# An attention and expert kernel: the work between the two expert stages moved, and the gate's iterations cut in parts

## The chip, the cores and the metric

The kernel runs on one core of one Trainium2 chip. The metric is the device time of one execution in microseconds (us); the median of three runs counts. One more execution was profiled, and all rows below are from it. The engines are called as the profile calls them: PE is TensorE (matrix products), DVE is VectorE, ACT is ScalarE, POOL is GpSimd, and SP only starts transfers. PEld is the loading of weights into TensorE, which runs beside its matmuls.

## What is computed

The reference has three parts in a row, on 1152 tokens of 512 values. Attention with a learned bias gives x; a dense layer with softplus follows; then comes a mixture of eight experts, whose gate is a matrix of probabilities that is normalized by rows and by columns eight times.

```python
# dense layer: w_in 512 x 2048, w_out 2048 x 512
h = x @ w_in
x = softplus(h) @ w_out
# experts: w1[e] 512 x 1024, w2[e] 1024 x 512
P = np.exp(x @ w_gate - (x @ w_gate).max())      # 1152 x 8
for _ in range(8):
    P /= P.sum(1, keepdims=True) + 1e-09
    P /= P.sum(0, keepdims=True) + 1e-09
    P *= N / E
out = 0
for e in range(8):
    out += P[:, e:e + 1] * (np.maximum(x @ w1[e], 0.0) @ w2[e])
```

## The kernel before

Everything is in fp32. A product is made of three matmuls on a high and a low part of each operand (`TRIPS`), so each operand must first be split: ACT copies it to the high part, and DVE or POOL subtracts that to get the low part.

The dense layer and the experts are cut into 40 **units** of 256 hidden columns. Units 0 to 7 are the dense layer (`U1` is 8); units 8 to 39 are the experts, four units (`UE`) for each, so that units 8 to 11 are expert 0. All emission is by hand: `unit(u)` writes the instructions of one unit in the order in which each engine will run them, and each engine runs its own list in order. Tiles and semaphores only add the waits.

The tokens are two chunks of 512 (c = 0 and 1) and a rest of 128. A unit of the experts has these steps on PE. First come seven block products of x with w1 in the order 1, 2, 6, 7, 5, 3, 4 (a Strassen scheme over 2 x 2 blocks; product 6 needs the block sum S2, product 7 needs S3, 5 needs S1, 3 needs S4, and 4 needs the plain block A22). Then `up_last` does the 128 rest tokens, `down(u, 0)` and `down(u, 1)` multiply the hidden values with w2, four matmul groups (i = 0 to 3) each, and `down_last` does the rest. After each group DVE adds the result to the output tile `acc` (`evac`). PSUM has eight banks: two called `t`, one `tail`, one `pv`, and two double ones called `s`, which hold the sums of `down`.

The block sums are needed in the experts alone, and they are sums of the dense layer's output, so they can only be made when unit 7 ends. `x_next` and `finish_x` do this: `x_mix` adds two blocks of 128 x 512, on DVE or POOL, and `x_split` makes the high part on ACT and the low part on DVE or POOL. `x_part` splits a plain block (A11, A12, A22). `rows_to_x` transposes the rest tokens on PE and splits them.

The gate is a list of closures: logits, transposes to tokens, the maximum, the exponential, and eight iterations `columns(it)`. Each iteration is a matmul with a matrix of ones on PE, into bank `pv`, and nine small DVE instructions on tiles `prob` (128 x 72), `r8` and `r9`. `ask()` takes the next closure off the list. It is called six times in each unit from unit 8 on, so that the 17 closures are used up in units 8 to 10. From expert 1 on (unit 12), `acc` is first scaled by expert 0's probability (`weigh`, nine DVE instructions).

POOL mainly prepares the weights: `mix` makes sums of weight blocks and `parts` splits weights (ACT copies, L613; POOL subtracts, L614). `JOBS` says after which step of a unit the weights of the next unit are made.

Of the kernel before, what the change touches and what calls it, by code (L numbers as in the profile page):

```python
# [24 lines left out]
E = 8  # L25
# [62 lines left out]
def attention_moe_moe_kernel(ctx: ExitStack, tc, qT, kT, vN, wpos, w_in, w_out, w_gate, e_w1, e_w2,  # L88
# [421 lines left out]
    def experts(m0, accp, xr):  # L510
# [247 lines left out]
        def down(u, c):  # L758
            w = wd(u).rearrange("p o (t f) -> p o t f", t=2)
            order = (0, 2, 1, 3) if u == U1 - 1 else (0, 1, 2, 3)  # L760
            t = [ps2("sum") for _ in range(2)]
            for i, k in enumerate(order):
# [11 lines left out]
                if i == 1 and u >= U1:  # L774
                    ask()
# [3 lines left out]
        def down_last(u):  # L779
            w = wd(u).rearrange("p o (t f) -> p o t f", t=2)  # L780
            r, n, t = bank("pv"), 0, h["last"]
# [4 lines left out]
            evac(u, 2, 0, r)  # L786
            if u == U1 - 1:
                finish_x()
# [19 lines left out]
        def x_next(c, k):  # L808

            if c == 0:  # L810
                xsrc[0] = acc[0]
                x_part("A11" if k < 2 else "A12", k % 2)
                return
            xsrc[1] = acc[1]
            if k == 2:
                x_mix("S1", 0, nc.gpsimd)
            elif k == 3:
                for n in range(2):
                    x_mix("S3", n, nc.gpsimd)
                x_mix("S2", 0)  # L820
                x_mix("S1", 1)
                x_mix("S2", 1)

        def finish_x():
            for k in range(2):
                x_split("S2", k, nc.vector)
            for name in ("S3", "S1"):
# [60 lines left out]
        def exps():  # L888
            mb = bank("pv")
# [3 lines left out]
            rows()  # L893

        def rows():
            nc.vector.tensor_reduce(pool["r9"], pool["prob"], axis=AX.X, op=ALU.add)
            nc.vector.tensor_scalar(pool["r9"], pool["r9"], 1e-9, None, ALU.add)
            nc.vector.reciprocal(pool["r9"], pool["r9"])
            nc.vector.tensor_tensor(out=pool["prob"], in0=pool["prob"], in1=pool["r9"].rearrange("p (t o) -> p t o", o=1).to_broadcast(
                [128, NTOK // 128, E]), op=ALU.mult)  # L900

        def columns(it):
            cs = bank("pv")
            nc.tensor.matmul(cs[:, 0:NTOK // 128 * E], ones, pool["prob"].rearrange("p t e -> p (t e)"), start=True, stop=True)
            nc.vector.tensor_reduce(pool["r8"], cs[:, 0:NTOK // 128 * E].rearrange("p (t e) -> p e t", e=E), axis=AX.X, op=ALU.add)
            nc.vector.tensor_scalar(pool["r8"], pool["r8"], 1e-9, None, ALU.add)
            nc.vector.reciprocal(pool["r8"], pool["r8"])
            nc.vector.tensor_scalar(pool["r8"], pool["r8"], float(NTOK / E), None, ALU.mult)
            nc.vector.tensor_tensor(out=pool["prob"], in0=pool["prob"], in1=pool["r8"].rearrange("p (o e) -> p o e", o=1).to_broadcast(
                [128, NTOK // 128, E]), op=ALU.mult)  # L910
            if it < 7:
                rows()

        def weigh():

            for t in range(NTOK // 128):
                d = acc[t // 4][:, t % 4]
                nc.vector.tensor_scalar(d, d, pool["prob"][:, t, 0:1], None, ALU.mult)

        gate = []  # L920
        for c in range(3):
# [258 lines left out]
```

## Time and profile before

| | us |
|---|---|
| median of 3 runs (1289.26 to 1289.4) | 1289.33 |
| the profiled execution's own time | 1289.71 |
| its span on the core | 1287.8 |
| PE busy in the span | 1203.0 (93%) |
| DVE busy | 841.1 (65%) |
| POOL busy | 581.6 (45%) |
| ACT busy | 488.3 (38%) |

The span is the time from the first to the last instruction of the profiled execution, and 1.9 us lie around it. Times in the rows count from the start of the span. A row's last part in square brackets is how long the engine sat idle before the instruction, and on what it had waited. [...]

### The profile page before, as it was taken

The numbers are of one execution on the slowest core, as the hardware profiler recorded it, in microseconds if no ns is written. First come the engines' busy times: TensorE is split into PE (matmuls) and PEld (weight loads), VectorE is DVE, ScalarE is ACT, GpSimd is POOL, SyncE is SP. The second block draws the span as 40 slices with busy tenths as digits, with TensorE's granted clock in tenths as the row PEclk, the third lists the DMA queues.
The fourth block names the chain that finished last, engine by engine and source line by source line (L and its number), as shares of the span: only waits on it lengthen the run. The fifth ranks groups of instructions, "written<-read, shape, count | busy, mean of one in ns | idle before, by whom it ended". The sixth has DMA issues, their size and how long they took to land.

```text
span 1287.8 us, 19090 instructions
## 1 busy us (share of the span) xinstructions
PE 1203.0 (93%) x7460; PEld 1011.3 (79%) x7460; DVE 841.1 (65%) x1502; ACT 488.3 (38%) x855; POOL 581.6 (45%) x452
## 2 busy tenths in 40 slices
PE   5775989999999998988999999999999999999998
PEld 4675868887887885766888888888888888888887
DVE  8883678764777766377756556656566566565665
ACT  7773766784332333322323223223232232232321
POOL 1122677655444549333534534544445345444440
PEclk9887999999999998999999999999999999999999
DMA  4998636603222311110111111111111111111101
GB/s 92 147 195 170 182 84 205 184 2 98 81 83 77 108 46 33 33 41 26 48 49 50 50 33 50 50 33 49 50 50 49 33 50 50 33 49 50 33 1 74
DMA packets 75148, 90.85 MB, mean 71 GB/s; under 512 B 17332, under 2 KB 51764, under 8 KB 75060
## 3 DMA queue, kind: packets, MB, share of 16 engines
q1 hardware_dynamic: 74772, 89.36, 25.6%
q8 instruction: 58, 0.95, 0.3%
q14 instruction: 30, 0.25, 0.1%
q10 hardware_dynamic: 288, 0.30, 0.1%
HBM read 74.45 MB, written 15.19 MB: 70 GB/s over the span
## 4 chain that ended last, share of the span: by engine, by line
PE 77%; DVE 11%; DMA 4%; POOL 3%; issue 2%; ACT 2%; SPq 1%; POOLq 0%; DVEq 0%; ACTq 0%
PE sum L770 31%; PE t L676 16%; PE pv L784 4%; PE tail L744 3%; PE pv L676 3%; PE tail L676 3%; PE t L691 3%; PE op L449 2%; PE pac L198 2%; PE pv L691 1%; PE tail L691 1%; PE sps L361 1%; PE tp L412 1%; DVE m L188 1%; DVE acc L800 1%
## 5 line engine op out<-in xcount | busy, mean ns | idle before, releaser
L614 POOL TENSOR_TENSOR wu<-f,wu 128x1024 fp32r<-128x1024 f32 x72 | 172.8, 2400 | 445.0 <-ACT wu L613 444.5
L770 PE MATMUL sum<-wd,h 128*128 128x512 f32 x1536 | 367.1, 395 | 1.5 <-DVE acc L800 1.5
L770 PEld LDWEIGHTS sum<-wd,h 128*128 128x128 f32 x1536 | 285.9, 190 | 59.1 <-DVE acc L800 2.0
L802 DVE SCALAR_TENSOR_TENSOR acc<-sum,prob,acc 128x512 f32<-128x512 f32 x224 | 168.2, 751 | 137.4 <-PE sum L770 137.4
L676 PE MATMUL t<-room,wu 128*128 128x512 f32 x512 | 142.4, 390 | 2.7 <-ACT v L726 2.7
L676 PE MATMUL t<-x,wu 128*128 128x512 f32 x448 | 122.6, 390 | 0.0
L676 PEld LDWEIGHTS t<-room,wu 128*128 128x128 f32 x512 | 95.9, 188 | 22.9 <-ACT v L726 3.1
L614 POOL TENSOR_TENSOR wd<-f,wd 128x1024 fp32r<-128x1024 f32 x40 | 96.0, 2399 | 36.5 <-ACT wd L613 36.5
L726 ACT ACTIVATE v<-t 128x512 f32<-128x512 f32 x32 | 19.1, 597 | 242.9 <-PE t L676 242.9
L198 PE MATMUL pac<-bw,m 128*128 128x64 bf16 (+1 forms) x1920 | 72.5, 204 | 32.6 <-DVE bw L171 12.3
L676 PEld LDWEIGHTS t<-x,wu 128*128 128x128 f32 x448 | 84.2, 188 | 17.5
L198 PEld LDWEIGHTS <-m 128*128 128x128 bf16 (+1 forms) x1920 | 69.1, 109 | 35.8 <-issue 26.6
L770 PE MATMUL sum<-h,wd 128*128 128x512 f32 x384 | 94.1, 397 | 2.7 <-DVE acc L800 2.0
L770 PEld LDWEIGHTS sum<-h,wd 128*128 128x128 f32 x384 | 69.9, 188 | 21.6 <-DVE acc L800 7.1
L613 ACT ACTIVATE wu<-f 128x1024 fp32r<-128x1024 f32 x72 | 75.8, 1053 | 15.6 <-DVE f L595 15.6
L579 POOL TENSOR_SCALAR f<-f 128x512 f32<-128x512 f32 x32 | 61.8, 1939 | 28.3 <-DVE f L578 28.0
L800 DVE TENSOR_TENSOR acc<-sum,acc 128x512 f32<-128x512 f32 x80 | 54.6, 687 | 27.7 <-PE sum L770 27.2
L378 ACT ACTIVATE p<-p,sm 128x576 f32<-128x576 f32 x72 | 55.7, 773 | 31.8 <-DVE sm L374 20.7
L711 ACT ACTIVATE hl<-tail 128x256 fp32r<-128x256 f32 x40 | 15.3, 384 | 130.6 <-PE tail L753 130.6
L374 DVE CUSTOM_DVE_ANT_0 p<-sps,bias 128x576 f32<-128x576 f32 x72 | 54.0, 750 | 15.9 <-DMA bias<-wt 10.8
L711 ACT ACTIVATE h<-pv 128x512 fp32r<-128x512 f32 x40 | 23.9, 598 | 103.1 <-DVE pv L695 102.8
L695 DVE TENSOR_TENSOR tail<-tail,v 128x512 f32<-128x512 f32 x32 | 22.4, 699 | 60.9 <-PE tail L676 60.3
(188 smaller groups left out, 2180.4 us busy)
## 6 DMA issues: line engine op xcount, KB each, us to landing
f<-in_e_w_dram SPq DMA_DIRECT2D x128, 256.0 KB, 2.9
raw<-in_w_in_dram SPq DMA_DIRECT2D x16, 512.0 KB, 3.7
raw<-in_w_out_dram SPq DMA_DIRECT2D x16, 512.0 KB, 3.6
wt<-extra SPq DMA_DIRECT2D x10, 512.0 KB, 7.7
raw<-in_qT_dram SPq DMA_DIRECT2D x16, 288.0 KB, 4.9
raw<-in_kT_dram SPq DMA_DIRECT2D x16, 288.0 KB, 4.5
bias<-wt SPq DMA_DIRECT2D x16, 288.0 KB, 4.6
bias<-wt SPq DMA_DIRECT2D x16, 256.0 KB, 4.4
```

What stands on the lines that cost most here:

```text
L198: nc.tensor.matmul(pt[0:n, g], lhs, win(w, (k * (ng + 1) + gw) * NC, [[(ng - gw) * NC, 2], [1, NC]]), start=(k == 0), stop=(k == 2))
L374: nc.vector.tensor_tensor_reduce(out=p.rearrange("p (a j) -> p a j", a=2), in0=sps[:, :, 0:288], in1=bias.rearrange("p (a j) -> p a j", a= ...
L378: nc.scalar.activation(p, p, AF.Exp, bias=sm[:, o:o + 1], scale=-1.0, accum_out=sm[:, 2 + o:3 + o])
L579: nc.gpsimd.tensor_scalar(t, t, F64_MIN, F64_MAX, ALU.max, ALU.min)
L613: nc.scalar.activation(w[:, 0], src, AF.Copy)
L614: nc.gpsimd.tensor_tensor(out=w[:, 1], in0=src, in1=w[:, 0].bitcast(F32), op=ALU.subtract)
L676: nc.tensor.matmul(z[n], wu(u)[:, a, o:o + 128], xs[xn][b][j], start=(k == 0), stop=(k == 5))
L691: nc.tensor.matmul(zz, wu(u)[:, a, o:o + 128], xs[f"A{c + 1}{k // 2 + 1}"][b][k % 2], start=(k == 0 and n == 0), stop=(k == 3 and n == 2))
L770: nc.tensor.matmul(s, lhs, rhs, start=(n == 0), stop=(n == 5))
L784: nc.tensor.matmul(r, t[:, b, 128 * f:128 * f + 128], w[:, a, f], start=(n == 0), stop=(n == 5))
L800: nc.vector.tensor_tensor(out=d, in0=o, in1=d, op=ALU.add)
L802: nc.vector.scalar_tensor_tensor(out=d, in0=o, scalar=pool["prob"][:, t, e:e + 1], in1=d, op0=ALU.mult, op1=ALU.add)
```

## The change

There are three edits, and some small ones that go with them.

**The block sums.** All of `x_mix` is now on DVE, and its pieces stand between the last evictions of unit 7 and the first of unit 8, in the order in which the products need them: S2, S3, S1, S4. All low parts of the sums are made on DVE too; A22 stays on POOL. The rest tokens' sum of unit 7 goes into a bank of `s` (`sumr`) instead of `pv`, and it is evicted later. `rows_to_x` comes after product 3 instead of product 5, as one instruction on each engine instead of four. The weights of unit 8 are made earlier in unit 7 (`FIRST`).

**The gate.** Each iteration is three closures instead of one, each with a named place in a unit: r0 to r2 around `up_last`, a0 to a3 after the four evictions of `down(u, 0)`, and b0 to b3 after those of `down(u, 1)`. The intermediate values stand in the bank `pv` instead of SBUF. The multiplication by N / E is folded into the one that follows it. The last iteration now comes in unit 12.

**The weighting** of `acc` in unit 12 is nine ACT instructions instead of nine on DVE, each group just ahead of the sums that need it.

```diff
         def down(u, c):
+            weigh(u, c)
...
                 evac(u, c, k, s)
                 convert(1)
-                if i == 1 and u >= U1:
-                    ask()
+                ask(u, "ab"[c] + str(i))
...
         def down_last(u):
-            r, n, t = bank("pv"), 0, h["last"]
+            weigh(u, 2)
+            r, n, t = bank("pv") if u != U1 - 1 else ps2("sumr")[:, 0], 0, h["last"]
...
-            evac(u, 2, 0, r)
             if u == U1 - 1:
-                finish_x()
+                pool["sumr"] = r
+            else:
+                evac(u, 2, 0, r)
...
             if k == 2:
-                x_mix("S1", 0, nc.gpsimd)
+                x_mix("S1", 0)
+            elif k == 1:
+                x_mix("S2", 0)
             elif k == 3:
-                for n in range(2):
-                    x_mix("S3", n, nc.gpsimd)
-                x_mix("S2", 0)
                 x_mix("S1", 1)
                 x_mix("S2", 1)
-
-        def finish_x():
...
+                for n in range(2):
+                    x_split("S2", n, nc.vector)
+                for n in range(2):
+                    x_mix("S3", n)
+
+        def finish_x(n):
+            if n == 1:
                 for k in range(2):
-                    x_split(name, k)
-            for k in range(2):
-                x_mix("S4", k)
-                x_split("S4", k, nc.vector)
-            for k in range(2):
-                x_part("A22", k)
+                    x_split("S3", k, nc.vector)
+                evac(U1 - 1, 2, 0, pool.pop("sumr"))
+            elif n == 2:
+                for k in range(2):
+                    x_split("S1", k, nc.vector)
+            elif n == 6:
+                for k in range(2):
+                    x_mix("S4", k)
+                for k in range(2):
+                    x_split("S4", k, nc.vector)
+            elif n == 7:
+                for k in range(2):
+                    x_part("A22", k)
+            elif n == 3:
+                rows_to_x()
...
         def columns(it):
...
+            def first():
+                cs["t"] = t = bank("pv")
...
+                nc.tensor.matmul(t[:, 0:NT * E], ones, pool["prob"].rearrange("p t e -> p (t e)"), start=True, stop=True)
+                r8 = t[:, 256:256 + E]
+                nc.vector.tensor_reduce(r8, t[:, 0:NT * E].rearrange("p (t e) -> p e t", e=E), axis=AX.X, op=ALU.add)
+                nc.vector.tensor_scalar(r8, r8, 1e-9, None, ALU.add)
+                nc.vector.reciprocal(r8, r8)
...
+            def second():
...
+                if it < 7:
+                    rows(cs["p"], cs["t"][:, 300:300 + NT])
+
+            def third():
+                if it < 7:
+                    rows_done(cs["p"], cs["t"][:, 300:300 + NT], pool["r9"])
...
+        for it, (n, at) in enumerate(((1, "b"), (2, "r"), (2, "a"), (2, "b"), (3, "r"), (3, "a"), (3, "b"), (4, "r"))):
+            for k, fn in enumerate(columns(it)):
+                gate[n, f"{at}{k}"] = fn
...
+        FIRST = {0: (("mix", 0),), 1: (("high", 0),), 2: (("high", 1),), 3: (("highd", 0),)}
```

How the lists of the engines move is shown at three places. A row has the line, the operation, the tile that is written and those that are read, and the shape.

The first place is DVE from the last evictions of unit 7 into the first products of unit 8. `raw_2551` is S1, `raw_2552` S2, `raw_4620` S3 and `raw_4621` S4; `x_4625`, `room`, `x_4623` and `x_4627` are the low parts of S2, S3, S1 and S4. Before:

```order
L713 TENSOR_TENSOR hl<-tail,hl 128x256
L800 TENSOR_TENSOR acc<-sum,acc 128x512 x4
L651 TENSOR_TENSOR raw_2552<-raw_2551,acc 128x512
L651 TENSOR_TENSOR raw_2551<-acc 128x512
L651 TENSOR_TENSOR raw_2552<-raw_2551,acc 128x512
L800 TENSOR_TENSOR acc<-pv,acc 128x512
L656 TENSOR_TENSOR x_4625<-raw_2552,x_4624 128x512 x2
L651 TENSOR_TENSOR raw_4621<-acc,raw_2552 128x512
L656 TENSOR_TENSOR x_4627<-raw_4621,x_4626 128x512
L651 TENSOR_TENSOR raw_4621<-acc,raw_2552 128x512
L656 TENSOR_TENSOR x_4627<-raw_4621,x_4626 128x512
```

And now:

```order
L651 TENSOR_TENSOR raw_2552<-raw_2551,acc 128x512
L656 TENSOR_TENSOR x_4625<-raw_2552,x_4624 128x512 x2
L651 TENSOR_TENSOR raw_4620<-acc 128x512 x2
L656 TENSOR_TENSOR room<-raw_4620,room 128x512 x2
L802 TENSOR_TENSOR acc<-sumr,acc 128x512
L695 TENSOR_TENSOR tail<-tail,v_6120 128x512
L886 COPY lgt<-pv 8x512
L656 TENSOR_TENSOR x_4623<-raw_2551,x_4622 128x512 x2
L695 TENSOR_TENSOR u_6166<-t,v_6120 128x512
L715 SCALAR_TENSOR_TENSOR h<-tail,h 128x512
L651 TENSOR_TENSOR raw_4621<-acc,raw_2552 128x512 x2
L656 TENSOR_TENSOR x_4627<-raw_4621,x_4626 128x512 x2
```

The sums of S3 (which POOL made) and the low parts of S3 and S1 (also POOL's) have come into this list, and the eviction of the rest tokens has moved behind S3. Above this piece, between the last three evictions of unit 7, stand the first halves of S1 and S2 and the second half of S1.

The second place is POOL over the same stretch, from the high blocks' low parts (`room<-acc`: A11 and A12) to those of A22 (`x_4628`). Before:

```order
L637 TENSOR_TENSOR room<-acc,room 128x512 x4
L614 TENSOR_TENSOR wd_2548<-f_4618,wd_2548 128x1024
L651 TENSOR_TENSOR raw_2551<-acc 128x512
L651 TENSOR_TENSOR raw_4620<-acc 128x512 x2
L656 TENSOR_TENSOR room<-raw_4620,room 128x512 x2
L656 TENSOR_TENSOR x_4623<-raw_2551,x_4622 128x512 x2
L637 TENSOR_TENSOR x_4628<-acc,room 128x512 x2
```

And now:

```order
L637 TENSOR_TENSOR room<-acc,room 128x512 x4
L607 TENSOR_TENSOR f_2550<-f_4617 128x2x2x128
L608 TENSOR_TENSOR f_2550<-f_4617 128x2x128
L609 TENSOR_TENSOR f_2550<-f_4617,f_2550 128x2x128
L610 TENSOR_TENSOR f_2550<-f_2550 128x2x128
L614 TENSOR_TENSOR wu_4615<-f_4617,wu_4615 128x1024
L637 TENSOR_TENSOR x_4628<-acc,room 128x512 x2
```

The seven rows of S1 and S3 are gone. In front of A22 there now stand the weight sums of unit 9 (L607 to L610) and the split of its first weights (L614), which waits for ACT's copy of the same weights; on ACT that copy (L613, `wu_4615<-f_4617`) stands behind the high parts of S4.

The third place is DVE around `up_last` of unit 10, where one gate iteration stands behind product 4 and ahead of the first eviction of `down`. Before:

```order
L695 TENSOR_TENSOR t<-t,u_6641 128x512
L715 SCALAR_TENSOR_TENSOR h<-t,h 128x512
L905 TENSOR_REDUCE r_5177<-pv 128x8
L906 TENSOR_SCALAR r_5177<-r_5177 128x8
L907 RECIPROCAL r_5177<-r_5177 128x8
L908 TENSOR_SCALAR r_5177<-r_5177 128x8
L909 TENSOR_TENSOR prob<-prob,r_5177 128x72
L896 TENSOR_REDUCE r_5176<-prob 128x9
L897 TENSOR_SCALAR r_5176<-r_5176 128x9
L898 RECIPROCAL r_5176<-r_5176 128x9
L899 TENSOR_TENSOR prob<-prob,r_5176 128x72
L715 SCALAR_TENSOR_TENSOR h<-t,h 128x512
L800 TENSOR_TENSOR acc<-sum,acc 128x512 x2
```

And now:

```order
L695 TENSOR_TENSOR t<-t,u_6611 128x512
L715 SCALAR_TENSOR_TENSOR h<-t,h 128x512
L929 TENSOR_REDUCE pv<-pv 128x8
L930 TENSOR_SCALAR pv<-pv 128x8
L931 RECIPROCAL pv<-pv 128x8
L935 SCALAR_TENSOR_TENSOR pv<-prob,pv 128x72
L912 TENSOR_REDUCE pv<-pv 128x9
L913 TENSOR_SCALAR pv<-pv 128x9
L715 SCALAR_TENSOR_TENSOR h<-t,h 128x512
L916 RECIPROCAL r_5176<-pv 128x9
L917 TENSOR_TENSOR prob<-pv,r_5176 128x72
L802 TENSOR_TENSOR acc<-sum,acc 128x512
```

The nine small rows are now eight, with a low part of the hidden values (`h<-t,h`) among them, and all of them read `pv`, the PSUM bank; only the last two write to SBUF. The next iteration's matmul on PE (a0) stands behind the first group of `down(u, 0)` and reads the `prob` that the last small row writes.

## Rows read from the trace of the kernel before

**Rows 1.** Stretch, length, busy PE, PEld, DVE, ACT, POOL, PEclk: units 8 (halved) to 11.

```profile
495.79:521.62 25.83, 18.34 (x75) 12.39 (x74) 19.94 (x27) 11.10 (x21) 18.94 (x14) 0.87 0.13 42
521.62:539.22 17.60, 16.91 (x88) 12.24 (x86) 1.66 (x5) 7.25 (x13) 8.14 (x6) 1.00 0.10 31
539.22:569.62 30.40, 27.30 (x120) 21.55 (x120) 20.47 (x47) 8.22 (x12) 10.50 (x7) 0.94 0.10 35
569.62:602.61 32.99, 27.44 (x123) 21.95 (x122) 27.77 (x70) 6.49 (x10) 10.37 (x7) 0.95 0.10 33
602.61:626.07 23.46, 23.46 (x111) 19.63 (x110) 13.96 (x21) 6.49 (x10) 10.50 (x7) 1.00 0.13 45
```

**Rows 2.** What PE waited for from 478 to 626 us: total, times, longest.

```profile
PE pv L904 <- DVE prob L899: 4.3, 2, 2.5
...
PE pv L877 <- ACT acc L798: 0.7, 1, 0.7
```

**Rows 3.** Timeline of PE: start, duration, instructions, idle time before and its releaser.

```profile
491.57 3.02 PE L770 MATMUL sum<-h,wd 128*128 128x512 f32 x12 [0.76 <-DVE acc L800]
...
501.44 4.39 PE L870 MATMUL pv<-room,gw 128*8 128x512 f32 x12 [2.77 <-DVE acc L800]
...
509.92 1.65 PE L676 MATMUL t<-room,wu 128*128 128x512 f32 x6 [2.71 <-ACT v L726]
...
519.74 0.41 PE L877 MATMUL pv<-ident,lgt 8*128 8x8 f32 x4 [2.02 <-DVE h L715]
...
589.03 0.41 PE L904 MATMUL pv<-prob,ones 128*128 128x72 f32 x2 [2.48 <-DVE prob L899]
```

**Rows 4.** Short stretches behind three waits of PE, columns as in rows 1.

```profile
502.50:504.50 2.00, 2.00 (x6) 0.63 (x5) 1.77 (x2) 1.22 (x3) 2.00 (x2) 0.50 0.04 8
...
520.00:522.00 2.00, 2.00 (x17) 1.94 (x16) 1.67 (x4) 1.62 (x3) 0.00 (x0) 1.00 0.15 50
...
590.50:592.50 2.00, 2.00 (x6) 1.52 (x6) 1.83 (x7) 0.00 (x0) 1.59 (x3) 0.50 0.55 207
```

**Rows 5.** Timeline of DVE and POOL where both work on SBUF.

```profile
495.29 4.22 POOL L651 TENSOR_TENSOR raw<-acc 128x512 f32<-128x512 f32 x3
...
498.30 1.76 DVE L651 TENSOR_TENSOR raw<-acc 128x512 f32<-128x512 f32 x1
...
500.09 0.69 DVE L651 TENSOR_TENSOR raw<-raw,acc 128x512 f32<-128x512 f32 x1
...
586.45 2.34 POOL L614 TENSOR_TENSOR wd<-f,wd 128x1024 fp32r<-128x1024 f32 x1
586.56 0.22 DVE L898 RECIPROCAL r<-r 128x9 f32<-128x9 f32 x1
586.81 2.07 DVE L899 TENSOR_TENSOR prob<-prob,r 128x72 f32<-128x72 f32 x1
```

**Rows 6.** Groups by line and shape, 495.79 to 626.07 us: count, busy us, mean ns.

```profile
L614 POOL TENSOR_TENSOR wu<-f,wu 128x1024 fp32r<-128x1024 f32 x8 | 19.2, 2398 | 56.5 <-ACT wu L613 56.5
...
L613 ACT ACTIVATE wu<-f 128x1024 fp32r<-128x1024 f32 x8 | 8.4, 1052 | 0.0
...
L607 POOL TENSOR_TENSOR f<-f 128x512 f32<-128x512 f32 x5 | 6.4, 1288 | 0.0
...
L637 POOL TENSOR_TENSOR x<-acc,room 128x512 fp32r<-128x512 f32 x2 | 2.8, 1420 | 0.1
...
L896 DVE TENSOR_REDUCE r<-prob 128x9 f32<-128x72 f32 x8 | 1.8, 230 | 0.7 <-ACT prob L892 0.4
...
L905 DVE TENSOR_REDUCE r<-pv 128x8 f32<-128x72 f32 x8 | 1.8, 223 | 0.5 <-PE pv L904 0.5
```

**Rows 7.** Timeline of PE and DVE in unit 11, from the end of product 4.

```profile
612.13 1.59 PE L744 MATMUL tail<-wu,xl 128*128 128x256 f32 x12
...
612.93 1.45 DVE L715 SCALAR_TENSOR_TENSOR h<-t,h 128x512 fp32r<-128x512 f32 x2
...
613.56 2.68 PE L770 MATMUL sum<-wd,h 128*128 128x512 f32 x11
```

More of the change, by code (lines that the diff above doesn't have):

```diff
@@ L892, in exps @@
             nc.scalar.activation(pool["prob"], pool["prob"], AF.Exp, bias=pool["mx"][:, 2:3])
[L893 to L900, printed above, removed]
@@ L902, in columns @@
-        def columns(it):
[L903 to L921, printed above, removed]
-            gate += [lambda c=c: logits(c), lambda c=c: tokens_down(c)]
-        gate += [max_rows, max_all, exps]
-        gate += [lambda it=it: columns(it) for it in range(8)]
+        NT = NTOK // 128
+        def rows(src, r9):
+            nc.vector.tensor_reduce(r9, src, axis=AX.X, op=ALU.add)
+            nc.vector.tensor_scalar(r9, r9, 1e-9, None, ALU.add)
@@ new lines, in weigh, with tokens_max @@
+        def weigh(u, c):
+            if u == U1 + UE:
+                for k in range(4 if c < 2 else 1):
+                    d = acc[c][:, k]
+                    nc.scalar.activation(d, d, AF.Copy, scale=pool["prob"][:, 4 * c + k, 0:1])
+        def tokens_max():
+            tokens_down(2)
+            max_rows()
+        gate = {(0, "p"): lambda: logits(0), (0, "r1"): lambda: tokens_down(0), (0, "a0"): lambda: logits(1),
+                (0, "a2"): lambda: tokens_down(1), (0, "b0"): lambda: logits(2), (0, "b2"): tokens_max,
+                (1, "r1"): max_all, (1, "a0"): exps, (1, "a2"): lambda: rows(pool["prob"], pool["mb"][:, 300:300 + NT]),
+                (1, "a3"): lambda: rows_done(pool["prob"], *[pool["mb"][:, 300:300 + NT]] * 2)}
@@ L997, in jobs @@
                 if U1 <= u + 1 < NU:
-                    for what, k in JOBS.get(n, ()):
+                    for what, k in (JOBS if u >= U1 else FIRST).get(n, ()):
                         weights[what](u + 1, k)
@@ L1033, in unit @@
                 return
-            if u == U1 + UE:
-                while gate:
-                    gate.pop(0)()
-                weigh()
             for n, p in enumerate((1, 2, 6, 7, 5, 3, 4)):
@@ L1040, in unit @@
                 jobs(n)
-                if n == (1 if u == U1 else 3) or n == 6:
-                    ask()
-                if u == U1 and n == 4:
-                    rows_to_x()
+                if n == 1:
+                    ask(u, "p")
+                if u == U1:
+                    finish_x(p)
+            ask(u, "r0")
             up_last(u)
+            ask(u, "r1")
             low()
+            ask(u, "r2")
             load_up()
@@ L1050, in unit @@
             jobs(8)
-            ask()
             turn_last(u)
@@ L1054, in unit @@
             down_last(u)
-            ask()
             load_down()
@@ L1063, in convert, with ask @@
                 weights[what](u, k)
-        def ask():
-            if gate:
-                gate.pop(0)()
+        def ask(u, at):
+            fn = gate.pop((u - U1, at), None)
+            if fn:
+                fn()
         return beside, rest
```

23 lines of the change are left out of this document (16 added, 7 removed).

## The prediction

> **What bounds the kernel now.** I read the stretches first. They show PE without a gap in unit 11: 23.46 us busy of 23.46, at the full clock [rows 1]. From unit 12 to the end the units keep that length, so nothing that lightens another engine there can shorten the run. The place to look is units 8 to 10, which take 25.83 + 17.60 + 30.40 + 32.99 = 106.82 us where three units like unit 11 would take 70.38 [rows 1]. This excess of 36.4 us is all that the change can work on. It has three parts.
>
> - PE stands idle for 7.5 + 0.7 + 3.1 + 5.6 = 16.8 us, the differences of span and busy time [rows 1]. The waits of PE say for whom: before logits it waits 2.77 us for the eviction on DVE that frees bank `pv`; then 2.71 for ACT's copy of product 1, late because ACT stands behind the splits of the block sums; then 2.02 for DVE [rows 3]. In units 9 and 10 it waits for `prob`, 4.3 us in two waits [rows 2].
> - PE has work of its own for the gate: two logits of 12 matmuls, small transposes, ones-matmuls. Eleven matmuls of 512 columns take 2.68 us with the tail [rows 7], so 12 take 2.75 and a product of 6 takes 1.36. With the rest chunk, the transposes of the rest tokens and the ones-matmuls I put all of it at 9.6. This stays.
> - The rest, 36.4 - 16.8 - 9.6 = 10 us, is work at the lower clock. [...] So a long wait is paid again behind it: busy time in a half-clock stretch counts double, and I value one such stretch at 2 us.
>
> **Unit 7's end and the products of unit 8.** I walk through the lists on the old trace's time axis. In the old list, group i = 2 of `down(7, 1)` waits 0.76 us [rows 3] for an eviction that is late because ACT copied weights (1.05 us, [rows 6]) just before the rest tokens' hidden values. That copy now comes earlier in the unit, under products that PE does anyway, and the 0.76 is gained. Product 1 then starts at about 494.9.
>
> The logits no longer wait for the rest tokens' sum, which now has a bank of its own. They run from 497.6 to 500.3, and product 6 wants S2 then. On DVE there stand, ahead of S2's low parts, two evictions, four sums and the splits; one op on 128 x 512 is 0.69 us undisturbed [rows 5].
>
> The price of these ops is open, because POOL works beside them. A sum with both inputs in SBUF took 1.76 us while POOL worked on three sums of its own, and 0.69 alone [rows 5]: up to 1.1 more for each. POOL's list now brings unit 9's weight sums at that time, from 490.8 on: one op of 1.29 us [rows 6] and three on half as much, 3.5 in all. So the disturbance costs nothing at best, and 4 x 1.1 = 4.3 at worst. I take 1.2, two sums that wait for the rest of one POOL op, since POOL's next piece stands still until ACT comes to its copy.
>
> [...]
>
> S2 is then ready at 498.1 and S3 at 500.7, both before PE wants them (500.3, 501.7). From there DVE is behind: eviction of the rest sum, product 2, logits copy, S1's low parts (ready at 504.4, wanted at 503), product 6, a low part, two sums S4, two splits: 19 ops from the second half of S1 on, at 0.65 each with the waits for ACT in between, end at 508.2. Product 3 ends at 508.6 where it would have ended at 505.8.
>
> Next late is A22. ACT copies unit 9's first weights after S4's high parts (to 508.5), POOL splits them (2.4 us, to 510.9), and only then come A22's two low parts (2.8 us with both, [rows 6]; 2.5 undisturbed), to 513.4. Product 4 ends at 514.0 and `up_last` at 515.4. In the old trace `up_last` ends at 521.62 [rows 1]. **This stretch gains 6.2 us**, the 0.76 included. The cover that is gone here is POOL's: before, A22 did not stand behind the weights.
>
> The holes of some 2 us before product 3 and 2.6 before product 4 may lower the clock behind them, as the old waits did. I count one such stretch, **2.0 lost** (bounds: 0, since 2.02 did nothing, and 4).
>
> **The rest of unit 8** loses its wait of 0.7 [rows 2], since the last transposes now come ahead of a matmul group instead of behind everything. One group of transposes (0.34) moves into it. **0.4 gained.**
>
> **Units 9 and 10.** All small ops now read PSUM, or SBUF with one operand only. The old trace shows why that matters: a `prob` update with both operands in SBUF took 2.07 us while POOL split weights, and a reciprocal beside the same POOL op took 0.22 [rows 5]. A small op costs 0.22 to 0.23 us whether its source is PSUM or SBUF [rows 6], so I put no price on PSUM.
>
> [...]
>
> The parts matter where PE waits for `prob`. Between a and b, and between b and the next r, there are 2 us or more of matmuls to spare after the third part. Between r and a there are not. In unit 11 product 4 ended at 612.13; DVE finished the first of two low parts at 613.6 [rows 7]. From there a chain of six small ops (0.26 from one to the next with the wait for itself), one low part (0.6) and two more small ops makes 2.5, to 616.1. The first group of `down` ends 0.4 later than in rows 7 because of the ones-matmul, at 615.3, so PE waits 0.85 there, and about 0.2 for bank `pv` at r0. That is 1.05 in each of units 10 and 11.
>
> Unit 9 gets 23.46 + 0.64 of PE work (maximum, broadcast, one iteration) + 0.2 = 24.3. Unit 10 gets 23.46 + 3 x 0.17 + 1.05 = 25.0. Together 49.3 against 63.4 [rows 1]: **14.1 gained**, waits of 1 us being too short for the lower clock by rows 3 and 4.
>
> **Units 11 and 12** now carry the last iterations. Unit 11 takes 25.0 instead of 23.46, **1.5 lost**; unit 12 **0.4 lost**, a ones-matmul and the wait for `pv`. The weighting moves from DVE, where PE never waited for it, to ACT, which is busy 6.49 us in such a unit [rows 1]: nine copies of 0.6 each (my estimate; one of twice the size takes 1.05, [rows 6]) finish one matmul group ahead of each eviction. Nothing gained or lost; without that cover each would delay an eviction by 0.6, which PE's spare bank would still hide.
>
> **The sum**: 6.2 - 2.0 + 0.4 + 14.1 - 1.5 - 0.4 = 16.8. From the profiled execution's 1289.71 this gives 1272.9, and I say 1273.0. The median of before lies 0.4 below its profiled execution, less than any term here.
>
> **Rivals.** (1) *Unit 8 keeps its length.* The waits for logits and product 1's copy go, but S4 and A22, later by POOL's disturbance at its bound of 4.3 and a second half-clock stretch, take their place: 6.2 - 2.0 + 0.4 becomes 0.4, and the time 1277.3. For it speaks that DVE takes eight ops that POOL did; against it that POOL has little to do until ACT comes.
>
> (2) *Unit 8 runs nearly freely.* No disturbance (1.2), no lower clock (2.0), DVE's ops end to end at 0.6 (1.0): 1268.8. For it: DVE's waits for ACT may hide under its own ops.
>
> (3) *The gate still stops PE.* If every r to a step also has another op that POOL holds for 2.1 us [rows 5], as unit 10 had, the two steps cost 4.2 and two half-clock stretches 4: 1281. Against it: no op of the new chain has two SBUF inputs.
>
> (4) *Slower than before.* One mechanism: an op with a single SBUF input is held by POOL as well. Then in each of the eight iterations the op that updates `prob` can lose 2.1 us in sight of PE. All eight together eat the 16.8, and only the half-clock stretches behind such waits (2 each) would put the run above before, at some 1295. Rows 5's reciprocal, undisturbed at 0.22 in the middle of a POOL op, is against it.
>
> That the change does nothing would need the excess to be PE's own work, and 16.8 us of it is idle time.
>
> **How the numbers follow.** Forecast 0.62, (1) 0.15, (2) 0.14, (3) 0.06, (4) 0.02, nothing 0.01. The forecast's own range is 1270.5 to 1276. To hold 8 in 10 and the bounds of disturbance and clock, it reaches from (2) to beyond (1): 1268 to 1278.5. Within 0.2% (2.6 us, about what a measurement of this kernel can tell from no change) lie only the last case and half of the fourth: faster 0.96, same 0.02, slower 0.02.
>
> **What would show it.** Product 1 to the start of `down(8, 0)` at about 20.5 us with its waits before products 3 and 4, the last one for A22 on POOL; no wait before the logits; units 10 and 11 at about 25 with one wait of 0.85 for `prob` behind the first group of `down`; no small op of the gate over 0.3 us; unit 12 like unit 13. The prediction fails most likely in unit 8: if DVE's new sums run at 1.76, or if the clock falls twice.

## The result, and the profile after

The changed kernel took 1271.14 us (median of four executions, 1268.3 to 1272.01) against 1289.37 for the kernel before in the same session (1289.26 to 1290.4). The ratio is 0.9854, with a 95% interval of 0.9837 to 0.9871. The forecast was 1273.0, in a range of 1268 to 1278.5. The profiled execution took 1270.74, its span is 1268.9.

First the same stretches as in [rows 1], and one more (columns: span, length, busy PE, PEld, DVE, ACT, POOL, then PEclk, the clock granted to PE as a share of its full speed): product 1 to `down(8, 0)`, the rest of unit 8, units 9, 10, 11, 12.

```profile
492.62:514.02 21.40, 17.98 (x75) 12.55 (x73) 17.04 (x27) 10.21 (x17) 4.89 (x4) 0.84 0.08 26
514.02:531.17 17.15, 17.15 (x88) 12.46 (x86) 2.76 (x8) 6.40 (x12) 8.13 (x6) 1.00 0.09 31
531.17:555.77 24.60, 24.60 (x117) 20.06 (x115) 15.57 (x34) 8.73 (x13) 10.55 (x7) 1.00 0.13 44
555.77:581.17 25.40, 24.89 (x117) 20.07 (x116) 18.32 (x45) 6.49 (x10) 10.47 (x7) 1.00 0.13 42
581.17:606.60 25.43, 24.91 (x117) 20.06 (x116) 18.33 (x45) 6.49 (x10) 10.48 (x7) 1.00 0.12 42
606.60:630.65 24.05, 23.96 (x114) 19.77 (x112) 15.02 (x25) 12.00 (x19) 10.56 (x7) 1.00 0.14 44
```

Against [rows 1] the first four stretches are 4.43, 0.45, 5.80 and 7.59 us shorter, and unit 11 is 1.97 longer. POOL's busy time in the first one falls from 18.94 to 4.89: its seven ops on S1 and S3 are now DVE's, and the weight sums of unit 9 come before this stretch. Next, what PE waited for between 478 and 626 us, to be held against [rows 2]:

```profile
PE t L676 <- ACT x L655: 1.6, 1, 1.6
PE t L676 <- POOL x L637: 1.6, 1, 1.6
PE pv L927 <- DVE prob L917: 0.9, 2, 0.4
PE t L676 <- DVE x L656: 0.2, 1, 0.2
```

The 4.3 us for `prob` [rows 2] have become 0.9, and the wait of 2.77 before the logits [rows 3] is gone. PE's timeline shows where the two long waits stand (start, duration, instructions, in brackets the idle time before and its releaser):

```profile
495.34 2.93 PE L884 MATMUL pv<-room,gw 128*8 128x512 f32 x12
...
504.14 0.50 PE L676 MATMUL t<-x,wu 128*128 128x512 f32 x1 [1.62 <-ACT x L655]
504.87 1.64 PE L676 MATMUL t<-x,wu 128*128 128x512 f32 x5 [0.23 <-DVE x L656]
...
509.37 0.80 PE L676 MATMUL t<-x,wu 128*128 128x512 f32 x1 [1.58 <-POOL x L637]
...
569.27 0.41 PE L927 MATMUL pv<-prob,ones 128*128 128x72 f32 x2 [0.43 <-DVE prob L917]
```

They stand before product 3 (S4) and inside product 4 (A22). Behind the first the clock falls; these short stretches have the columns of the first view and answer to [rows 4]:

```profile
504.00:506.00 2.00, 1.63 (x6) 1.14 (x7) 1.91 (x4) 2.00 (x4) 0.28 (x1) 0.98 0.00 0
506.00:508.00 2.00, 1.79 (x7) 1.08 (x5) 1.90 (x4) 1.23 (x3) 2.00 (x1) 0.50 0.01 4
508.00:510.00 2.00, 0.63 (x2) 0.54 (x3) 1.40 (x3) 1.13 (x3) 2.00 (x3) 0.50 0.31 98
510.00:512.00 2.00, 2.00 (x7) 1.51 (x6) 0.09 (x1) 0.00 (x0) 0.54 (x1) 0.50 0.47 164
512.00:514.00 2.00, 2.00 (x16) 1.86 (x15) 1.20 (x2) 1.30 (x2) 0.00 (x0) 0.81 0.00 0
```

From 506 to 512 PE is busy for 1.79 + 0.63 + 2.00 = 4.4 us at 0.50 of the clock; at full clock this would be some 2.2 us, so about 2.2 are lost. Here are DVE and POOL beside each other where the prediction left the price of a sum open [rows 5]:

```profile
489.34 0.84 DVE L651 TENSOR_TENSOR raw<-acc 128x512 f32<-128x512 f32 x1
...
490.71 0.68 DVE L651 TENSOR_TENSOR raw<-raw,acc 128x512 f32<-128x512 f32 x1
...
492.19 1.04 DVE L651 TENSOR_TENSOR raw<-acc 128x512 f32<-128x512 f32 x1
...
488.34 1.30 POOL L607 TENSOR_TENSOR f<-f 128x512 f32<-128x512 f32 x1
489.59 1.20 POOL L608 TENSOR_TENSOR f<-f 128x256 f32<-128x256 f32 x1
490.74 1.24 POOL L609 TENSOR_TENSOR f<-f,f 128x256 f32<-128x256 f32 x1
491.94 0.74 POOL L610 TENSOR_TENSOR f<-f 128x256 f32<-128x256 f32 x1
```

The two sums that are lengthened at all take 0.84 and 1.04, not 1.76. Where one of these sums of DVE and an op of POOL meet, the one that starts second pays. DVE's at 489.34 meets POOL's of 488.34 and takes 0.84; POOL's at 489.59 meets DVE's and takes 1.20, and the one at 490.74, 0.03 behind DVE's undisturbed 0.68, takes 1.24. POOL's at 491.94 starts ahead of DVE's of 492.19: it takes its undisturbed 0.74, and DVE's takes 1.04. Last, the gate's small ops, grouped by line (count, busy us, mean ns):

```profile
L912 DVE TENSOR_REDUCE pv<-pv 128x9 f32<-128x72 f32 x7 | 1.7, 242 | 0.2
...
L917 DVE TENSOR_TENSOR prob<-pv,r 128x72 f32<-128x72 f32 x7 | 1.6, 232 | 0.2
L935 DVE SCALAR_TENSOR_TENSOR pv<-prob,pv 128x72 f32<-128x72 f32 x7 | 1.6, 230 | 0.1
...
L913 DVE TENSOR_SCALAR pv<-pv 128x9 f32<-128x9 f32 x8 | 1.4, 174 | 0.3
...
L912 DVE TENSOR_REDUCE pv<-prob 128x9 f32<-128x72 f32 x1 | 0.2, 226 | 0.0
```

None is held any more. The reduction takes 242 ns from PSUM (`pv`) and 226 from SBUF (`prob`).

### The profile page after: what moved, and what is told of

Read it like the earlier page. It is cut to its first block, busy times and chain, and to the rows that moved or that the text cites. A ratio compares the mean times of both kernels' runs of the same rounds, so it can differ in the third digit from the quotient of the medians.

```text
span 1268.9 us, 19083 instructions
## 1 busy us (share of the span) xinstructions
PE 1198.1 (94%) x7460; PEld 1007.5 (79%) x7460; DVE 829.5 (65%) x1489; ACT 493.2 (39%) x861; POOL 571.7 (45%) x445
## 4 chain that ended last, share of the span: by engine, by line
PE 79%; DVE 9%; DMA 5%; ACT 2%; issue 2%; POOL 2%; SPq 1%; POOLq 0%; DVEq 0%
PE sum L771 33%; PE t L676 16%; PE pv L785 4%; PE tail L744 3%; PE pv L676 3%; PE tail L676 3%; PE t L691 3%; PE op L449 3%; PE pac L198 2%; PE tail L691 2%; PE pv L691 2%; PE sps L361 1%; DMA bias<-wt 1%; DVE m L188 1%; PE tp L412 1%
## 5 line engine op out<-in xcount | busy, mean ns | idle before, releaser
L614 POOL TENSOR_TENSOR wu<-f,wu 128x1024 fp32r<-128x1024 f32 x72 | 172.8, 2400 | 440.2 <-ACT wu L613 440.2
L614 POOL TENSOR_TENSOR wd<-f,wd 128x1024 fp32r<-128x1024 f32 x40 | 96.0, 2401 | 37.2 <-ACT wd L613 29.2
L613 ACT ACTIVATE wu<-f 128x1024 fp32r<-128x1024 f32 x72 | 75.8, 1053 | 15.6 <-DVE f L595 15.6
```

The source lines that it names most:

```text
L613: nc.scalar.activation(w[:, 0], src, AF.Copy)
L614: nc.gpsimd.tensor_tensor(out=w[:, 1], in0=src, in1=w[:, 0].bitcast(F32), op=ALU.subtract)
```

## The experiments

The stages ahead of unit 0 hold code that no run here changes, and yet the start of unit 0's `up_last` lies between 294.13 and 301.61 us in the fourteen profiles; from there to unit 7's it is 179.2 to 179.4 in all of them. Differences of a few us between whole times therefore say little. I judge by the **core stretch**: on PE from the start of unit 7's `up_last` to that of unit 13's, cut at those of units 8, 9 and 12. All in us, from each kernel's own profile; median and ratio are over four to eleven executions of each kernel, the ratio to the kernel before on the same chip.

| kernel | median | ratio, 95% | 7 to 8 | 8 to 9 | 9 to 12 | 12 to 13 | whole |
|---|---|---|---|---|---|---|---|
| before | | | 39.30 | 29.07 | 86.44 | 23.48 | 178.29 |
| the change | 1271.14 | 0.9854 (0.9837-0.9871) | 33.13 | 29.02 | 75.92 | 23.56 | 161.63 |
| again | 1271.48 | 0.9869 (0.9849-0.9889) | 33.14 | 29.10 | 75.90 | 23.56 | 161.70 |
| sums_only | 1283.69 | 0.9950 (0.9931-0.9968) | 33.77 | 31.23 | 86.54 | 23.49 | 175.03 |
| gate_only | 1275.58 | 0.9900 (0.9881-0.9919) | 36.67 | 28.72 | 75.91 | 23.55 | 164.85 |
| gate_sbuf | 1282.44 | 0.9947 (0.9926-0.9967) | 33.13 | 29.14 | 86.55 | 23.54 | 172.36 |
| one_piece | 1273.21 | 0.9881 (0.9859-0.9902) | 33.09 | 29.31 | 77.59 | 23.53 | 163.52 |
| weigh_dve | 1281.10 | 0.9934 (0.9912-0.9956) | 33.10 | 29.16 | 75.94 | 32.98 | 171.18 |
| a22_early | 1269.92 | 0.9849 (0.9829-0.9869) | 33.02 | 28.56 | 75.90 | 23.56 | 161.04 |
| s4_early | 1272.07 | 0.9869 (0.9846-0.9891) | 33.55 | 28.67 | 75.90 | 23.55 | 161.67 |
| mix_first | 1264.94 | 0.9836 (0.9817-0.9854) | 31.40 | 30.12 | 75.88 | 23.56 | 160.96 |
| mix_first_s4 | 1265.48 | 0.9845 (0.9818-0.9871) | 31.21 | 28.63 | 75.97 | 23.55 | 159.36 |
| r_joined | 1268.16 | 0.9860 (0.9841-0.9880) | 33.12 | 29.02 | 75.01 | 23.55 | 160.70 |
| all_three | 1265.29 | 0.9839 (0.9822-0.9857) | 31.19 | 28.63 | 75.04 | 23.55 | 158.41 |

**again**: the changed kernel once more, unedited.

> The changed kernel itself, once more. Measured from the up_last of unit 7 to the up_last of unit 13, the profiled execution of before took 178.3 us and that of the change 161.6. Theory: the change's whole gain lies in this stretch, so it comes out at 161.6 within 0.3 again, and the 2.2 us by which the changed kernel reached unit 7 earlier are chance in the attention stage, whose code is the same: the time to unit 7 will differ again by a microsecond or two, either way. Rival: the change also makes the stages ahead of unit 7 faster, then unit 7's up_last starts at 478.5 again and not near 480.8.

The core stretch came out at 161.70 beside 161.63, while unit 7's `up_last` started at 479.22 instead of 478.54. The stretch is repeatable to 0.1 us, and the change's gain lies in it: 16.66 of the 18.97 between the two profiled executions. 2.24 more lie ahead of unit 7's `up_last` (480.78 and 478.54), where the code is the same. That they are chance is likely from the spread and not shown: the one profile of before has the latest start of the fourteen, and in twelve of the thirteen rows below it the medians' gain on before is larger than the gain of the core stretch (over all thirteen by 1.3 us in the mean, 4.4 at most).

### The two halves of the change

**sums_only** has the new block sums with the old list of the gate, its old small ops and its old weighting; **gate_only** the reverse. A few lines of each, against the changed kernel:

```diff
 sums_only:
-                ask(u, "ab"[c] + str(i))
+                if i == 1 and u >= U1:
+                    ask()
...
 gate_only:
-                x_mix("S1", 0)
-            elif k == 1:
+                x_mix("S1", 0, nc.gpsimd)
+            elif k == 3:
+                for n in range(2):
+                    x_mix("S3", n, nc.gpsimd)
...
```

> The block sums and the rest tokens as in the change, the gate's list and the weighting as before. Theory: the two parts of the change do not touch each other, and this one is worth what unit 7's end and unit 8's products lost, 40.8 to 35.5 us from unit 7's up_last to the start of down in unit 8: 5 to 6 us faster than before, and units 9 to 12 as long as before (30.4, 33.0, 23.5). Rival: the gain of unit 8 hangs on the gate's new places too (the logits of chunk 0 and their transposes stand among the products); then less than 3 us are gained.

> The gate in parts with its values in PSUM and the weighting on ACT as in the change, the block sums as before. Theory: units 9 and 10 go from 63.4 to 50.0 us, units 11 and 12 lose 2.2, unit 8 gains 0.5: 11 to 12 us faster than before. Together with the block sums alone this makes the whole change. Rival: the parts share something, then the two alone add up to something else than 16.7, by more than 1 us.

The core stretch was 3.26 and 13.44 shorter than before; together 16.70, beside the 16.66 of the whole change. But sums_only gave less than the 5 to 6 expected and gate_only a little more than 11 to 12, and in both the clock has a part in it, so that the agreement to 0.04 is partly luck. In gate_only the way from unit 7 to 8 alone is 2.63 shorter. Here are a stretch of the kernel before and its product 5, then product 5 of gate_only:

```profile
512.00:514.00 2.00, 2.00 (x6) 1.43 (x6) 0.96 (x2) 0.17 (x1) 2.00 (x3) 0.50 0.00 0
...
511.41 2.72 PE L676 MATMUL pv<-x,wu 128*128 128x512 f32 x6
...
508.94 1.54 PE L676 MATMUL pv<-x,wu 128*128 128x512 f32 x6
```

Behind its wait of 2.71 [rows 3] the kernel before lost the full clock a second time in unit 8; behind the same wait, 2.58 in gate_only, the clock stayed at 1.00 (from 504 to 516). From product 5's start to product 3's that is 3.22 us against 1.73, or 1.49 of the 2.63, and nothing in the edit was meant to do it. The wait of 2.02 before the transposes [rows 3], which I had put under the sums, came from the old list's order: the transposes now stand behind `up_last`, which waits 1.29. In sums_only the way from 7 to 8 is 5.53 shorter, but 2.16 come back from 8 to 9, where the half-clock stretch now lies. These are its short stretches, columns as above:

```profile
511.00:513.00 2.00, 1.72 (x5) 0.93 (x5) 0.44 (x1) 0.00 (x0) 1.14 (x1) 0.72 0.74 248
513.00:515.00 2.00, 2.00 (x10) 1.64 (x10) 1.51 (x4) 0.76 (x2) 0.00 (x0) 0.50 0.00 0
515.00:517.00 2.00, 2.00 (x10) 1.92 (x10) 0.57 (x1) 0.89 (x2) 1.14 (x1) 0.50 0.00 0
```

### PSUM, parts, and who weights

**gate_sbuf** keeps the three parts and puts the values between the small ops into SBUF.

```diff
-                cs["p"] = t[:, 128:128 + NT * E].rearrange("p (t e) -> p t e", e=E)
+                cs["p"] = pool["cp"]
...
-                r8 = t[:, 256:256 + E]
+                r8 = pool["r8"]
...
-                    rows(cs["p"], cs["t"][:, 300:300 + NT])
+                    rows(cs["p"], pool["r9"])
```

> The change, but the gate's intermediate values (row sums, column sums and the scaled matrix) stand in SBUF tiles instead of the PSUM bank; places and parts as in the change. [...] Rival: the places alone make the gain; then within 1 us of the change.

It lost 10.7 us, where I had estimated 3 to 8 and the rival 1 at most: units 9 to 12 take 86.55, as long as before the change (86.44). DVE's timeline of this kernel, and below it POOL's:

```profile
600.15 2.31 DVE L913 TENSOR_SCALAR r<-r 128x9 f32<-128x9 f32 x1
602.38 0.68 DVE L715 SCALAR_TENSOR_TENSOR h<-t,h 128x512 fp32r<-128x512 f32 x1
602.98 0.20 DVE L916 RECIPROCAL r<-r 128x9 f32<-128x9 f32 x1
603.22 1.61 DVE L917 TENSOR_TENSOR prob<-cp,r 128x72 f32<-128x72 f32 x1
...
600.08 2.36 POOL L614 TENSOR_TENSOR wu<-f,wu 128x1024 fp32r<-128x1024 f32 x1 [4.33 <-ACT wu L613]
602.39 2.35 POOL L614 TENSOR_TENSOR wd<-f,wd 128x1024 fp32r<-128x1024 f32 x1
```

Two of the ops end with the POOL op beside them: the product of two SBUF operands, and also a TENSOR_SCALAR with a single SBUF source on 9 elements, 2.31 us where it takes 0.17 from PSUM. The reciprocal, one SBUF source too, runs through POOL's op in 0.20. PE then waits 3.9 us for `prob` twice over (7.8 in all), and the clock is 0.50 in the six us from 604.

**one_piece** keeps PSUM and issues each iteration as one part.

```diff
-            for k, fn in enumerate(columns(it)):
-                gate[n, f"{at}{k}"] = fn
+            gate[n, f"{at}0"] = lambda parts=columns(it): [fn() for fn in parts]
```

> The change, but each gate iteration is written in one piece at its first place (r0, a0 or b0) instead of in three parts; the values stay in PSUM. Theory: with short ops the chain is some 2.2 us, it delays one eviction by about 1 us, and PE has a whole group to spare: within 1 us of the change, or even 0.5 to 1 faster, since no low part stands in the chain between r0 and a0. Rival: the parts are what helps, and a chain in one piece ahead of an eviction stops PE as in the kernel before: 3 to 8 us slower than the change.

The stretch grew by 1.9, between the theory's 1 at most and the rival's 3 to 8. PE no longer waits for `prob`, because the chain is done earlier when no low part stands in it; but it waits five times, 1.6 in all, for evictions that stand behind the eight small ops:

```profile
PE sum L771 <- DVE acc L802: 1.6, 5, 0.4
```

Of the 1.9, 0.29 lie from unit 8 to 9, ahead of the first iteration, where the edit changes nothing. So PSUM carries most of the gate's gain (10.7), and the cutting is worth 1.7.

**weigh_dve** puts the weighting by expert 0's probability back on DVE, at its new place.

```diff
-                    nc.scalar.activation(d, d, AF.Copy, scale=pool["prob"][:, 4 * c + k, 0:1])
+                    nc.vector.tensor_scalar(d, d, pool["prob"][:, 4 * c + k, 0:1], None, ALU.mult)
```

> The change, but the nine scalings of acc in unit 12 run on DVE at the same places instead of on ACT. Theory: DVE has 0.4 us for each of them, as the 3.65 us for nine before show, and unit 12 stays as long within 0.5 us: no measurable difference. Rival: four of them behind the last iteration and ahead of the first eviction hold PE up by 1 us or more.

This theory fell: 9.5 us lost, 9.4 of them from unit 12 to 13, where 0 was expected. DVE's timeline, then POOL's:

```profile
619.95 7.10 DVE L952 TENSOR_SCALAR acc<-acc,prob 128x512 f32<-128x512 f32 x4
...
634.43 1.67 DVE L952 TENSOR_SCALAR acc<-acc,prob 128x512 f32<-128x512 f32 x4
...
619.62 2.40 POOL L614 TENSOR_TENSOR wu<-f,wu 128x1024 fp32r<-128x1024 f32 x1 [4.33 <-ACT wu L613]
621.99 2.52 POOL L614 TENSOR_TENSOR wd<-f,wd 128x1024 fp32r<-128x1024 f32 x1
624.47 1.44 POOL L607 TENSOR_TENSOR f<-f 128x512 f32<-128x512 f32 x1
```

In the same kernel, what PE waited for in the end, an eviction behind them:

```profile
PE sum L771 <- DVE acc L804: 6.3, 2, 5.8
```

Most of the other 3 us are the clock behind that wait: the next twelve matmuls take 5.49 us (the clock is 0.57 from 629 to 634), and the twelve after them 2.98 (1.00 from 634 on). Four such scalings take 7.10 us beside POOL and 1.67 while POOL rests. Before the change they came at 626.88, nine in 3.65 us, with POOL idle: by the place, not by the engine, they cost nothing. As in gate_sbuf (2.31 us for one on 9 elements), it is a TENSOR_SCALAR on SBUF that ran long beside POOL; I had expected that of ops with two SBUF inputs alone.

### The two waits that are left in unit 8

**a22_early** splits A22 before the rest sum's eviction, so that it stands ahead of unit 9's weights on ACT and POOL. **s4_early** also makes S4 and its high parts with S1's, its low parts later.

```diff
 both, in finish_x:
             if n == 1:
...
+                for k in range(2):
+                    x_part("A22", k)
...
-            elif n == 7:
-                for k in range(2):
-                    x_part("A22", k)
...
 s4_early:
-            elif n == 6:
...
+                    nc.scalar.activation(hi, src, AF.Copy)
+                    lows.insert(k, lambda hi=hi, lo=lo, src=src: nc.vector.tensor_tensor(
+                        out=lo, in0=src, in1=hi.bitcast(F32), op=ALU.subtract))
```

> The change, with one thing moved: the split of the plain block A22 (ACT copies, POOL subtracts) is written right behind the splits of S3, so that on POOL it stands ahead of unit 9's first weights instead of behind them. Theory: product 4 waits for nothing but POOL's list; it took 4.7 us from its first matmul to up_last instead of 1.4, so the stretch from unit 7's up_last to unit 13's gets 2.5 to 3.3 us shorter than 161.6. Rival: the two more copies on ACT push the high parts of S1 and S4 back by 1.1 us, product 5 or 3 waits instead, and less than 1 us is left.

> The change with A22's split moved as in the run before, and S4 moved too: its two sums stand on DVE right behind the low parts of S1, with the high parts on ACT behind them, and its low parts stand ahead of the low part of the hidden values. Theory: product 3, which waited 1.6 us for S4's high part, starts about 1.2 us earlier, on top of what A22's move gives: 3.5 to 4.5 us shorter than the change between the up_lasts of units 7 and 13. Rival: the eviction of product 6, now behind two sums, holds the bank that product 3 writes to; then no more is gained than with A22 alone.

The wait for POOL is gone in both, yet the stretch is only 0.6 shorter in the first and the same in the second, against 2.5 to 4.5 expected. DVE's and POOL's timelines of a22_early show a collision:

```profile
499.51 2.98 DVE L656 TENSOR_TENSOR x<-raw,x 128x512 fp32r<-128x512 f32 x2 [0.61 <-ACT x L655]
...
499.50 1.30 POOL L607 TENSOR_TENSOR f<-f 128x512 f32<-128x512 f32 x1
500.75 1.18 POOL L608 TENSOR_TENSOR f<-f 128x256 f32<-128x256 f32 x1
501.90 1.18 POOL L609 TENSOR_TENSOR f<-f,f 128x256 f32<-128x256 f32 x1
```

POOL's sums of unit 9's weights, at 488.34 in the changed kernel, now stand behind A22 and fall on S1's low parts: 2.98 for two where 1.29 is the undisturbed time. s4_early collides in the same way (2.96 for these two, and 2.34 for S4's two sums). The early place of POOL's sums was a cover that I had not named. It is not the whole reason: in a22_early the clock is also at 0.50 from 504 to 510, under products 3 and 4.

**mix_first** therefore also moves these sums to the start of unit 8; **mix_first_s4** is s4_early with the same edit.

```diff
+        SECOND = {0: (("mix", 0),), 3: (("high", 0),), 6: (("high", 1),), 8: (("highd", 0),)}
...
-                    for what, k in (JOBS if u >= U1 else FIRST).get(n, ()):
+                    for what, k in (JOBS if u > U1 else FIRST if u < U1 else SECOND).get(n, ()):
```

> The change with A22's split early, and with unit 9's weight sums on POOL kept where the change has them, ahead of A22 (they are written after product 1 instead of product 2). The run with A22 early alone had moved these sums to where DVE makes S1's low parts. Theory: it was that collision which took the gain away (two low parts took 2.98 us instead of 1.29, and S4 came 0.9 later); without it S1's low parts take 1.3 again, product 3 starts 3.3 us after product 5 as in the change, product 4 follows without a wait, and the stretch from unit 7's up_last to unit 13's is 2 to 3 us shorter than the change's 161.6; half-clock work behind the wait for S4 keeps it from more. [...]

> As the run before, with S4's sums and high parts written behind S1's low parts too. Theory: product 3 starts some 0.7 us earlier, and with all waits under 1.5 us the clock may stay full: 3 to 4.5 us shorter than the change's 161.6. Rival: product 3 waits for the eviction of product 6 behind the two sums, and nothing is added to the run before.

The collision is gone (two low parts take 1.29 again). mix_first is 1.73 shorter from 7 to 8, with the clock at 1.00 there (494 to 506), but behind a wait of 1.79 before `up_last` it is 0.57 from 506 to 510, in `down(8, 0)`, and 1.10 are lost from 8 to 9: 0.67 in all, less than the 2 to 3 expected. Its 160.96 lies 0.08 from a22_early, though the lower clock is now behind product 4 and not on it. So the collision alone did not hold A22's gain: without it PE reaches `up_last` sooner and waits there for the rest tokens' low part. mix_first_s4 is 2.27 shorter than the change (3 to 4.5 expected) and 2.31 shorter than s4_early, which has the collision. Its two parts have the full clock throughout:

```profile
476.16:507.37 31.21, 27.92 (x128) 20.60 (x126) 24.10 (x38) 14.72 (x25) 18.79 (x13) 1.00 0.15 51
507.37:536.00 28.63, 28.63 (x144) 22.15 (x144) 9.03 (x18) 11.42 (x19) 10.53 (x7) 1.00 0.09 25
```

What it gains is the half-clock stretch of 2.2 us (PE is busy for 27.92 + 28.63 us here and for 58.73 over the same two parts of the changed kernel), not the waits: PE's idle time from 7 to 8 is 31.21 - 27.92 = 3.29 and was 33.13 - 29.71 = 3.42. A22's wait of 1.58 is replaced by one of 2.18 for the rest tokens' low part, which stands at the end of DVE's row; from 486.96 to 508.5 DVE has no gap over 0.61, so I take its work itself as the bound that is left there. The medians of both kernels are some 6 us under the change's, but that is mostly the time ahead of unit 7 (its `up_last` starts at 473.41 and 476.16), and the kernel before was faster in that session too, at 1286.63.

### One wait of the gate

**r_joined** lets the second and third part of the iteration at r run together.

```diff
+            fns = columns(it)
+            if at == "r":
+                fns = fns[0], lambda fns=fns: (fns[1](), fns[2]())
...
```

> The change, with the second and third part of the iteration at r joined ahead of the last low part of the hidden values. Theory: the wait of 0.43 us for prob at a0 in units 10 and 11 is that low part's 0.6 us, so both waits go and the stretch is 0.8 to 0.9 us shorter than 161.6; the evictions at a and b stay apart and do not wait as in the run with all iterations in one piece. Rival: the low part is needed as early as it was; then down of chunk 1 waits instead.

The waits of 0.43 for `prob` are gone; units 10 and 11 take 24.97 and 24.95 between their `up_last`, and the stretch is 0.93 shorter, as expected. **all_three** joins A22, S4, the weights' sums and this edit.

> A22 early with unit 9's weight sums first, S4 early, and the iteration at r joined. Theory: the three gains add, 4 to 5 us shorter than the change's 161.6, and a time of 1266 to 1268 against the change's 1271. Rival: they share the same waits and add up to less than 3 us.

The core stretch is 158.41, 3.22 under the changed kernel's (4 to 5 expected, short by mix_first's share): the 2.27 and 0.93 add up. Its ratio of 0.9839 lies under the change's 0.9854, but the intervals overlap, so the whole times do not show that it is faster; the stretch does.

## Why the prediction was right, step by step

The sum of 16.8 has 16.66 in the core stretch against it. That it is so close is luck in part: its terms, below, are off by 1.2 us to one side and by 1.4 to the other. The profiled execution took 1270.74 rather than 1272.9 because the stages ahead were 2.24 faster, which the sum does not have; their spread of some us is more than the error of the sum.

- **Unit 7's end and unit 8's products**: 6.2 - 2.0 = 4.2 gained by the sum. From unit 7's `up_last` to `down(8, 0)`, measured: 0.93 up to product 1 (where I had 0.76) and 4.43 behind it, 5.36 in all. Of the 1.2 more, half is A22, ready 0.6 earlier than I had it (510.55, moved by the 2.24 us I had 511.16), and half the clock, as said below. The places were right. Moved by the 2.24 us, I had product 1 at 492.7 (measured 492.62) and product 3's end at 506.4 (506.5); what waits last is A22 on POOL, as forecast. The holes are 1.85 before product 3 and 1.58 in product 4 against 2 and 2.6. The second is short because the slow clock in front of it has used up part of the wait. In one_piece and weigh_dve, where unit 8 has the same lists, the clock stays full up to there (the last five matmuls of product 3 take 1.43 and 1.42 us, in the changed kernel 1.64), and PE waits 2.40 and 2.42 for A22, while the way from 7 to 8 is as long (33.09 and 33.10, beside 33.13). The row of one_piece:

```profile
508.73 0.50 PE L676 MATMUL t<-x,wu 128*128 128x512 f32 x1 [2.40 <-POOL x L637]
```

- **The disturbance by POOL**, taken as 1.2 between 0 and 4.3, cost DVE (0.84 - 0.69) + (1.04 - 0.69) = 0.5. The 1.76 of [rows 5] stood beside POOL ops on 128 x 512, most of those here are on half as much.
- **The half-clock stretch**, 2.0 by the sum, a value put on stretches like those behind the waits of 2.77 and 2.48, where PE was granted 0.50: one, of 2.2, of which some 0.8 (2.40 - 1.58, an estimate) only shorten the wait for A22. It came behind waits of 1.62 and 0.23, shorter than the 2.02 behind which before kept 1.00 [rows 3, 4]. Behind the same pair of waits (1.62 to 1.65, and 0.22 or 0.23) the clock fell in again, gate_sbuf and r_joined too (the four transposes behind product 3 take 1.05 or 1.06 us there), and stayed full in sums_only, one_piece, weigh_dve and mix_first (0.60 us), to fall behind a later wait. So the length of a wait alone doesn't tell, and the count of one was luck between bounds of 0 and 4.
- **The rest of unit 8**: 0.45 gained, 0.4 forecast.
- **Units 9 and 10**: 24.60 and 25.40, with 24.3 and 25.0 forecast; 13.39 gained instead of 14.1. The wait between r and a was 0.43, not 0.85, and bank `pv` cost 0.1, not 0.2. But PE's own work in unit 10 is 24.89, not 23.46 + 0.51: three ones-matmuls cost 24.89 - 23.46 = 1.43 there, 0.48 each and not 0.17. I had priced its slot alone (0.14 to 0.24 from its start to the next one's) and not what it costs the groups on either side of it.
- **Unit 11 and 12**: 1.97 and 0.59 lost where I had 1.5 and 0.4, by the same price.
- **PSUM at no price**: the reduction's 242 and 226 ns differ by 16, or 0.1 us over the seven reductions, so no price was near enough.
- **One SBUF operand** was the step that was wrong as an argument, though not in the sum. I took an op that reads SBUF with one operand only as safe from POOL, by the reciprocal of [rows 5]. The trace of before had a row against it, just ahead of that reciprocal:

```profile
584.38 2.14 DVE L897 TENSOR_SCALAR r<-r 128x9 f32<-128x9 f32 x1
```

It ends with the POOL op beside it (584.09 to 586.49), and in the chain behind the longest wait for `prob` it took as long as the product of 2.07 that I named. gate_sbuf shows it again. The change escaped it because its TENSOR_SCALARs read PSUM.

- **The weighting**: "Nothing gained or lost" holds for ACT (four copies of 0.64 us each and no wait behind them). On DVE at the new place it costs 9.5, by weigh_dve, which I had not seen coming either, for the same reason.

Of the rivals, the first and second miss the stretch of unit 8 on either side, the third would have shown waits of 2 us for `prob`. The fourth, that POOL holds ops with one SBUF input too, is half true: gate_sbuf shows it for TENSOR_SCALAR (2.31 us) and not for RECIPROCAL. In the changed kernel every TENSOR_SCALAR of the chain reads PSUM, so nothing of it was seen. I had excluded it by the one row on a reciprocal. (The first rival's own terms give 1277.1, not 1277.3.)

What stays open: why the stages ahead differ from profile to profile with the same code, and why the clock falls behind one wait of 1.6 us and not behind another like it.

## What to carry to other kernels

Where GpSimd works steadily, keep the small VectorE ops of a serial chain in PSUM, and count TENSOR_SCALAR among those that it holds (2.31 us on SBUF beside POOL, 0.17 on PSUM): here that was worth 10.7 us, the cutting into parts 1.7. Before moving work past another engine's list, look at what that list will then run beside: A22's move brought POOL's sums onto DVE's low parts. And look at who waits next: without that collision the move was still worth only 0.7, since another wait took its place, and 2.3 with S4 moved too. Compare kernels that differ by a few us in the stretch that differs, and add a half-clock stretch for a wait only as a range.

## What had not been expected of the hardware

- Where DVE sums and POOL sums meet on SBUF, either engine can be the one that pays, by the order of starts: POOL's ops took 1.20 and 1.24 instead of 0.74, DVE's 0.84 and 1.04 instead of 0.69.
- A TENSOR_SCALAR on nine elements can take 2.31 us, and four on 128 x 512 can take 7.10 instead of 1.67.
- Where the lower clock lies behind a wait, and whether it comes at all, differed: in the changed kernel, after a wait of 1.62, it was 0.50 from 506 to 512, inside products 3 and 4; in mix_first, after one of 1.79, it was 0.57 from 506 to 510, in `down(8, 0)` (six matmuls of 512 columns in 2.88 us instead of 1.65); in mix_first_s4 a wait of 2.18 was followed by 1.00 (from 507.37 on).
